# Four modulation vectors moved from the tensor engine to the vector engine, with the first LayerNorm and the first loads reordered

## The chip, the cores and the metric

The kernel runs on one core of one Trainium2 chip. The metric is the device time of one execution in microseconds (us). Times are medians, with the range in brackets. The profile and the trace are those of one execution of each kernel, so a number read from them can differ from the median of the runs by a few tenths of a per cent.

Engines: PE is the tensor engine, ACT the scalar engine, DVE the vector engine, POOL is GpSimd, SP is the engine that only issues transfers. ACT can issue transfers too. In these traces an issue that takes long holds up what stands behind it on the same engine (9.59 us on ACT's queue, below). The granted clock is the share of PE's full clock that the profile records as allowed; at half clock it is 0.5 (so from 15 to 28 us in the kernel before).

## The reference, cut to what matters

```python
mod = (silu(c) @ w_mod).reshape(1, 6, 1, 640)      # c: 1x640, w_mod: 640x3840
sa, ca, ga, sb, cb, gb = mod[:, 0], ..., mod[:, 5]
h = layernorm(x) * (1 + ca) + sa                   # x: 2048x640
x = x + ga * attention(h, k_cache, v_cache, wq, wo)   # 32 heads of 128, 2048 keys
h = layernorm(x) * (1 + cb) + sb
x = x + gb * block_B(h)                            # a small gated MLP block
```

Attention is nearly all of the work: 32 heads times 4 chunks of 512 queries, 128 steps, each with 8 softmax exponentials of 128x1024. The vectors `sa` and `ca` are needed at once. The vectors `ga`, `sb`, `cb` and `gb` are needed only after most of the attention is done.

## The kernel before

The kernel does not write its instructions in program order. It records operations with an estimated duration and a priority, and a small planner at the top of the file simulates the five engines and decides the order in which each engine gets its instructions. Two of its lines are part of the change:

```python
            t_eng[e] = s + o.dur                      # when the engine is free again
            ...
            for u in o.succ:                          # when a successor may start
                u.ready = max(u.ready, (o.end if o in u.deps else o.start) + u.slack + (...))
```

The four late vectors are computed on PE: `silu(c)` is broadcast to 128 columns (`s_bc`), and each vector is ten matmuls, whose result stands on all 128 partitions at once. The vector `ga` is made in the first 30 us, the other three inside steps 17 to 22.

```python
    def modulation(p, hf, w_ap, w_t, pool, key, prio):
        ...
        for k in range(KT):
            P.op("PE", lambda e, k=k: e.matmul(m[:, 0:HD], s_bc[:, k, :], w_ap[:, k, sl], ...), ...)
        P.op("DVE", lambda e: e.tensor_scalar_add(out=mod[p][hf].ap, in0=m[:, 0:HD], ...), ...)
    ...
    dma("ACT", lambda e: e.dma_start(pre_ap, mod_src(2)), 800, ...)        # weights of ga, 800 KB
    ...
    load_v(0, -296.5, "ACT", after=(ln0[1],))                              # V of head 0, on ACT's queue
    ...  # for head 1:
            load_v(h, (-293, -290, -289.5)[h - 1], "ACT" if h == 1 else "SP", ...)
```

ACT's queue also issues the load of the second chunk of x (in `ln1`, called "the x load" below) and the rest of the first `wq`. On the same engine, behind these issues, stand two of the five copies that turn the first normalised chunk into `hT`, the input of the first query projection.

At the far end of the attention, DVE and POOL share the residual work. For chunks 2 and 3 the sum `x1 = tmp + xb` is on DVE, while POOL multiplies and adds other tiles in chains. Both inputs of these operations are in SBUF. The result `x1` is stored in the space of `hT`, so the profile shows the sum as `f_hT<-f_tmp,f_y`.

```python
                if hf:
                    tt("DVE" if ch > 1 else "POOL", x1[t].ap, w.ap, xb[t].ap, ALU.add, ...)
```

Of the kernel before, what the change touches and what calls it, by code (L numbers as in the profile page):

```python
# [40 lines left out]
class Plan:  # L41
# [3 lines left out]
    ENG = ("PE", "ACT", "DVE", "POOL", "SP")  # L45
    FIRST = {"PE": 100000, "ACT": 100000, "DVE": -6, "POOL": 100000, "SP": -5}
# [43 lines left out]
    def schedule(self):  # L90
# [20 lines left out]
        while len(self.all) < len(self.ops):  # L111
            best = None
            for e in self.ENG:
                st = []
                for o in avail[e]:
                    if e == "PE" and o is not pe[pe_i]:
                        continue
                    r = o.ready
                    if not all(free[t.pool] for t in o.newps):
                        continue  # L120
                    r = max([r] + [min(free[t.pool])[0] for t in o.newps])
                    st.append((max(r, t_eng[e]), o.prio, o.seq, o))
                if not st:
                    continue
                lim = min(st)[0] + 30.0
                c = min((x for x in st if x[0] <= lim), key=lambda x: x[1:3])
                if best is None or c[0] < best[0]:
                    best = c
            assert best is not None, ("stuck", pe[pe_i].prio, [d.eng for d in pe[pe_i].deps if not hasattr(d, "end")])
            s, o = best[0], best[3]  # L130
            e = o.eng
            avail[e].remove(o)
            if e == "PE":
                pe_i += 1
            for t in o.newps:
                b = min(free[t.pool])
                free[t.pool].remove(b)
                t.bank, t.ap = b[1], self.pools[t.pool][b[1]]
                for d in b[2]:
                    o.deps.setdefault(d, False)  # L140
            o.start = s
            t_eng[e] = s + o.dur
            self.busy[e] += o.dur
            if o.dma:
                t = max(dma_t[e], s + o.dur)
                both = min(max(0.0, max(dma_t[x] for x in self.ENG if x != e) - t), o.kb * 1024 / 190.0)
                dma_t[e] = t + both + (o.kb * 1024 - 190.0 * both) / 380.0
                o.end = dma_t[e] + 2000.0
            else:
                o.end = s + o.dur + o.lat  # L150
            o.idx = len(self.seq[e])
            self.seq[e].append(o)
            self.all.append(o)
            for pool, bank in o.gives:
                free[pool].append((o.end, bank, (o,)))
            for u in o.succ:
                u.ndep -= 1
                u.ready = max(u.ready, (o.end if o in u.deps else o.start) + u.slack + (1500.0 if o.dma and u.eng in ("DVE", "ACT") and not u.dma else 0.0))
                if u.ndep == 0:
                    avail[u.eng].append(u)  # L160
            for t in o.ptiles:
                left[t] -= 1
                if left[t] == 0:
                    last = {}
                    for r in t.refs:
                        if r.eng not in last or r.idx > last[r.eng].idx:
                            last[r.eng] = r
                    free[t.pool].append((max(r.end for r in t.refs), t.bank, tuple(last.values())))
# [104 lines left out]
def fast_path(nc, es, flag, A_x, A_k_cache, A_v_cache, A_wq, A_wo, B_w1, B_w2, B_w3, B_w4, c, w_mod, out):  # L273
# [8 lines left out]
    G4 = D // 4  # L282
# [119 lines left out]
    for i in range(NKV - 1):  # L402
        v_ones(i)
# [47 lines left out]
    P.op("POOL", lambda e: e.tensor_copy(s_bc.ap, c_f.ap.unsqueeze(2).to_broadcast([128, KT, 128])), 1000, (c_f,), (s_bc,), -290, lat=300)  # L451
    spin(50, -298)
    for k in range(KT):
        def mcol(e, k=k):
            for j in range(2 * KT):
                ins = e.matmul(mc[:, j:j + 1], wm_ap[:, k, j * 128:(j + 1) * 128], s_bf[:, k:k + 1],
                               start=(k == 0 and j == 0), stop=(k == KT - 1), skip_group_check=True)
                if k < KT - 1:
                    dummy(e, 1)
            return ins  # L460
        P.op("PE", mcol, 2 * KT * (85 if k < KT - 1 else 62), (wm[k], s_bf, ones), (mc,) + ((warm,) if k < KT - 1 else ()), -290 + k, accum=True)
# [23 lines left out]
    def ln_stats(src, src_t, g, i, prio, slack=0.0):  # L485
        s = st[n_st[0] % NST]
        n_st[0] += 1
        for hf in range(2):
            P.op("DVE", lambda e, hf=hf: e.bn_stats(s[:, hf * 6:hf * 6 + 6], src[:, hf * HD:(hf + 1) * HD]), 485, src_t, (s,), prio, slack=slack)  # L489
        P.op("DVE", lambda e: e.bn_aggr(mv_ap[g][:, i, :], s.ap), 200, (s,), (mvs[g][i],), prio)  # L490
# [29 lines left out]
    def normed(dst, dst_t, src, src_t, g, i, fp, prio):  # L520
        P.op("DVE", lambda e: e.tensor_scalar(out=dst, in0=src, scalar1=mv_ap[g][:, i, 0:1], scalar2=rs_ap[g][:, i:i + 1],
                                              op0=ALU.subtract, op1=ALU.mult),
             445, src_t + (mvs[g][i], rs[g]), (dst_t,), prio)
# [23 lines left out]
    def ln1(ch, prio):  # L547
        g = ln_slot()
        if ch == 1:
# [3 lines left out]
                640, (), xs + held, -296.7, after=(wm_load[3], ln0[1]))  # L553
# [3 lines left out]
        for a, z in ((0, 2), (2, 4)) if ch < 2 else ((0, 4),):  # L557
            for i in range(a, z):
                ln_stats(xs[i].ap, (xs[i],) + held, g, i, prio, 0.0 if ch == 0 else 2000.0)
            if ch == 0:  # L560
                ln0.append(rstd_act(g, a, z, prio - 100))
            else:
                rstd_dve(g, a, z, prio - 1)
            for i in range(a, z):
                normed(xn[i].ap, xn[i], xs[i].ap, (xs[i],) + held, g, i, False, prio - 1)
        raw = [T() for _ in range(4)]
        if ch == 0:
# [5 lines left out]
            for i in range(4):  # L573
                def tr(e, i=i):
                    for k in range(KT):
                        ins = e.transpose(hslice(k, i, i + 1), xn[i][:, k * 128:(k + 1) * 128], ident_t[:])
                    return ins
                P.op("PE", tr, 330, (xn[i], ident), (hp[0], hp[1], hq, hp[4]), (-286.6 if i < 2 else -280) + 0.1 * i, accum=True)
# [44 lines left out]
    def modulation(p, hf, w_ap, w_t, pool, key, prio):  # L623
        m = Tile(pool=pool)
        sl = slice(hf * HD, (hf + 1) * HD)
        for k in range(KT):
            P.op("PE", lambda e, k=k: e.matmul(m[:, 0:HD], s_bc[:, k, :], w_ap[:, k, sl], start=(k == 0), stop=(k == KT - 1)),  # L627
                 MM(HD), (s_bc,) + w_t, (m,), key(k), accum=True)
        P.op("DVE", lambda e: e.tensor_scalar_add(out=mod[p][hf].ap, in0=m[:, 0:HD], scalar1=1.0 if p == 4 else 0.0),
             490, (m,), (mod[p][hf],), prio)  # L630

    mod_src = lambda p: w_mod[:, p * D:(p + 1) * D].rearrange("(k p) n -> p k n", p=128)
    pre_ap = KV_t[:, (NKV - 1) * KVW:(NKV - 1) * KVW + KT * D].rearrange("p (k n) -> p k n", k=KT)
    pre_t = tuple(K[NKV - 1]) + (V[NKV - 1],)
    dma("ACT", lambda e: e.dma_start(pre_ap, mod_src(2)), 800, (wm[3],), pre_t, -297, after=(ln0[0],))
    for hf in range(2):
        modulation(2, hf, pre_ap, pre_t, "O%d" % hf, lambda k, hf=hf: 0.5 + hf + 0.01 * k, -50)
    v_ones(NKV - 1)
    load_v(0, -296.5, "ACT", after=(ln0[1],))

    def load_head(h):
# [3 lines left out]
        if h in (1, 2, 3):  # L645
            load_k(h, (-294, -291, -289)[h - 1], (wm[2],), () if h < 3 else from_slot(12))
            load_v(h, (-293, -290, -289.5)[h - 1], "ACT" if h == 1 else "SP", () if h == 1 else (wm[2],), after=(ln0[1],) if h == 1 else ())
# [15 lines left out]
    MS = 17  # L663
    for n, p in enumerate((4, 3, 5)):
        dma("SP", lambda e, n=n, p=p: e.dma_start(w_half[n % 2], mod_src(p)), 800, (), (W12[n % 2],) + (w2b if n == 1 else ()) + tuple(wm),
            MS * NP - 30 + n, from_slot((MS + 2 * n) * NP - 20))
        for hf in range(2):
            modulation(p, hf, w_half[n % 2], (W12[n % 2],) + (w2b if n == 1 else ()), "M",
                       lambda k, i=2 * n + hf: NP * (MS + i) + 4.65 + k, NP * MS - 60)

# [10 lines left out]

    def q_proj(s, keys):
        g, ch, hh = of_step(s)
        q = QT[s % 3]
        m = Tile(pool="M")
        for i, kk in enumerate((0, 2, 1, 4, 3)):
            P.op("PE", lambda e, i=i, kk=kk: e.matmul(m.ap, wq_t[g % 2][:, kk, hh * 128:(hh + 1) * 128], hT_t[ch][:, kk, :],  # L687
                                                      start=(i == 0), stop=(i == KT - 1)),
                 MM(QC), (wq[g % 2][hh], hT[ch][kk]), (m,), keys[i], accum=True)
        P.op("DVE", lambda e: e.tensor_copy(q.ap, m.ap), 690, (m,), (q,), s * NP - 90)  # L690
# [45 lines left out]
    def step(s):  # L736
# [11 lines left out]
        for j in range(NP):  # L748
# [4 lines left out]
            for r in range(2):  # L753
                kt = 2 * j + r
                P.op("PE", lambda e, sp=sp, r=r, kt=kt: e.matmul(sp[:, r * QC:(r + 1) * QC], K_ap[b][:, kt * 128:(kt + 1) * 128], q.ap, start=True, stop=True),  # L755
                     MM(QC), (K[b][kt // 4], q), (sp,), n + (0.307 if 9 <= s < 112 else 0.01) * r, accum=True)
# [96 lines left out]
    dma("SP", lambda e: e.dma_start(w_half[0], B_w1.rearrange("(k p) n -> p k n", p=128)), 800, (), (W12[0],), E)  # L853
    w2_rows = B_w2.rearrange("(g r) n -> r g n", g=4)
    dma("SP", lambda e: e.dma_start(w_half[1][:, 0:4, :], w2_rows[0:128]), 640, (), (W12[1],), E)
    for g in range(4):
        dma("SP", lambda e, g=g: e.dma_start(w_half[1][g * 32:(g + 1) * 32, 4, :], w2_rows[128:G4, g, :]), 40, (), (w2b[g],), E)
# [885 lines left out]
```

## Time and profile before

| what | value | where |
|---|---|---|
| time | 1386.88 us (1386.02 to 1386.93), 3 runs | times |
| span of the profiled run | 1386.3 us | page, head |
| PE busy | 1371.0 us, 99% | page, part 1 |
| longest PE wait | 6.6 us, for ACT's copies | waits |
| granted clock, 14 to 30 us | 0.57 | windows |

PE is the engine to watch. From the page of the kernel before, part 1 (busy us of each engine, share of the span, number of instructions) and part 4 (the chain that ended last, by engine):

```profile
PE 1371.0 (99%) x13128; PEld 944.9 (68%) x13128; DVE 540.3 (39%) x1402; ACT 1101.7 (79%) x1143; POOL 101.9 (7%) x89
...
PE 97%; DVE 2%; ACTq 1%; ACT 0%; issue 0%; POOL 0%; POOLq 0%
```

From the stretches view (window, its length, then for each engine the busy time and the number of instructions in the order PE, PEld, DVE, ACT, POOL, then the granted clock, the DMA share and GB/s):

```profile
14.00:30.00 16.00, 8.56 (x31) 3.57 (x32) 2.95 (x6) 4.54 (x6) 0.13 (x1) 0.57 1.33 212
...
160.00:235.00 75.00, 75.00 (x744) 52.49 (x742) 24.42 (x61) 63.16 (x62) 0.00 (x0) 1.00 0.39 89
...
1150.00:1215.00 65.00, 63.27 (x636) 43.68 (x635) 45.85 (x122) 55.30 (x75) 38.36 (x33) 1.00 0.31 69
```

PE is full from 30 us on. It is badly used only from 14 to 30 us, where it was busy for 8.56 of 16 us and at little more than half the clock. The reason is in the timeline of ACT (start, duration, line and operation; ACTq marks an issue):

```profile
7.90 0.39 ACTq L635 DMA_DIRECT2D f_KV<-in_w_mod_dram  x1
...
10.15 0.38 ACTq L552 DMA_DIRECT2D f_y<-in_A_x_dram  x1
10.57 9.59 ACTq L605 DMA_DIRECT2D f_KV<-in_A_v_cache_dram  x2
20.20 0.78 ACT L581 ACTIVATE f_hT<-f_O,f_small 128x512 bf16<-128x512 bf16 x1 [9.85 <-issue]
```

The other issues in this stretch took 0.38 to 0.54 us. The two V loads took 9.59 us together, of which the second took 8.99 (11.17 to 20.16), and the first `hT` copy of ACT began only when they were done. PE waited for it; the waits view of PE from 10 to 30 us says:

```profile
PE f_M L687 <- ACT f_hT L581: 6.6, 1, 6.6
```

(The numbers are the total, the count and the longest wait, in us.) The line view of the modulation's matmuls (count, then the shortest, median and longest duration in ns, first and last start) shows what the four vectors cost PE:

```profile
L627 PE MATMUL f_M<-f_W,f_sbc x30: 299/299/300, 183.6 to 238.2; 128*128 128x320 bf16 x30
...
L627 PE MATMUL f_O<-f_KV,f_sbc x10: 474/474/475, 24.1 to 27.4; 128*128 128x320 bf16 x10
```

The ten of `ga` fell in the half-clock stretch, the other thirty at full clock into steps 17 to 22.

Last, the tail, which matters later: the timelines of DVE and of POOL of the kernel before near 1187 us.

```profile
1184.69 4.54 POOL L528 TENSOR_TENSOR f_y<-f_y,f_mod 128x640 f32<-128x640 f32 x3
1189.34 2.18 POOL L536 TENSOR_SCALAR f_xn<-f_y,f_small 128x640 bf16<-128x640 f32 x2
1191.49 2.11 POOL L528 TENSOR_TENSOR f_y<-f_y,f_mod 128x640 f32<-128x640 f32 x1
...
1187.05 0.69 DVE L690 CAST f_PQ<-f_M 128x512 bf16<-128x512 f32 x1
...
1188.05 1.86 DVE L528 TENSOR_TENSOR f_hT<-f_tmp,f_y 128x640 bf16<-128x640 f32 x1
...
1190.87 1.32 DVE L528 TENSOR_TENSOR f_hT<-f_tmp,f_y 128x640 bf16<-128x640 f32 x1
```

DVE casts the next query tile (`f_PQ<-f_M`) first and does the sum of tile 8 after it. The sum took 1.86 us, although the same sum takes 0.82 us when POOL is idle. Nobody waits for the sum here, so it costs nothing. The next sum, at 1190.87, shows that the waiting goes both ways: it took 1.32 us, and POOL's operation beside it (1191.49) took 2.11 us where 1.54 is usual.

### The profile page before, as it was taken

What the parts mean: (1) busy time and instruction counts of PE and PEld (TensorE: products, weight loads), DVE (VectorE), ACT (ScalarE), POOL (GpSimd) and SP (SyncE); (2) the same over time, 40 slices, a digit from 0 to 9 for tenths busy, and PEclk for the clock granted to TensorE, in tenths of its full rate; (3) what the DMA queues carried; (4) which work ended last, traced back from release to release, by engine and by line L of the source; (5) the groups of instructions that cost most, each with busy time, mean ns of one, the idle gap of its engine ahead of it and who ended that gap; (6) DMA issues with size and microseconds to landing.
All of it is one profiled execution on the core that took longest, in us unless ns stands there. A gap on an engine that the chain in (4) does not pass through costs nothing.

```text
span 1386.3 us, 29857 instructions
## 1 busy us (share of the span) xinstructions
PE 1371.0 (99%) x13128; PEld 944.9 (68%) x13128; DVE 540.3 (39%) x1402; ACT 1101.7 (79%) x1143; POOL 101.9 (7%) x89
## 2 busy tenths in 40 slices
PE   7999999999999999999999999999999999999999
PEld 5667776777677777777777677777676766655665
DVE  4553323223322332333233323332333245897663
ACT  3988888888898889888988888888888888833322
POOL 0000000000000000000000000000333236500000
PEclk8999999999999999999999999999999999999999
DMA  9460624242223412051125122432226101331220
GB/s 233 98 124 24 122 79 94 35 88 54 47 35 56 86 32 50 19 97 32 43 36 107 35 47 36 73 69 47 55 51 134 38 17 24 105 83 20 57 49 31
DMA packets 259164, 88.91 MB, mean 64 GB/s; under 512 B 236689, under 2 KB 257746, under 8 KB 259026
## 3 DMA queue, kind: packets, MB, share of 16 engines
q1 hardware_dynamic: 252498, 82.92, 30.4%
q10 hardware_dynamic: 6528, 4.00, 1.3%
q8 instruction: 105, 1.72, 0.5%
q14 instruction: 33, 0.27, 0.1%
HBM read 43.48 MB, written 2.62 MB: 33 GB/s over the span
## 4 chain that ended last, share of the span: by engine, by line
PE 97%; DVE 2%; ACTq 1%; ACT 0%; issue 0%; POOL 0%; POOLq 0%
PE f_O L774 33%; PE f_S L755 32%; PE f_M L687 10%; PE f_M L712 10%; PE f_S L951 2%; PE f_M L951 2%; PE f_S L938 2%; PE f_O L938 2%; PE f_S L889 1%; PE f_S L912 1%; PE f_M L912 1%; ACTq L605 1%; PE f_O L889 1%; DVE f_small L489 0%; PE f_M L627 0%; PE f_S L431 0%
## 5 line engine op out<-in xcount | busy, mean ns | idle before, releaser
L757 ACT ACTIVATE f_PQ<-f_S 128x1024 bf16<-128x1024 f32 x1024 | 1041.3, 1024 | 147.5 <-PE f_S L755 134.6
L774 PEld LDWEIGHTS f_O<-f_KV,f_PQ 128*128 128x128 bf16 x8192 | 589.6, 98 | 231.6 <-DVE f_OO L783 2.1
L755 PE MATMUL f_S<-f_PQ,f_KV 128*128 128x512 bf16 x2048 | 727.8, 380 | 1.0 <-DVE f_PQ L690 0.8
L774 PE MATMUL f_O<-f_KV,f_PQ 128*128 128x129 bf16 x8192 | 712.9, 220 | 1.3 <-DVE f_OO L783 1.3
L720 DVE TENSOR_TENSOR f_y<-f_M,f_y 128x320 f32<-128x320 f32 x192 | 94.3, 491 | 536.4 <-PE f_M L712 536.4
L712 PE MATMUL f_M<-f_wo,f_OO 128*128 128x320 bf16 x992 | 272.8, 299 | 0.0
L755 PEld LDWEIGHTS f_S<-f_PQ,f_KV 128*128 128x128 bf16 x2048 | 197.0, 98 | 31.8 <-DVE f_PQ L690 1.5
L687 PE MATMUL f_M<-f_hT,f_wq 128*128 128x512 bf16 x640 | 176.8, 380 | 7.5 <-ACT f_hT L581 6.6
L712 PEld LDWEIGHTS f_M<-f_wo,f_OO 128*128 128x128 bf16 x992 | 96.1, 98 | 28.5
L690 DVE CAST f_PQ<-f_M 128x512 bf16<-128x512 f32 x128 | 88.4, 691 | 63.2 <-PE f_M L687 63.1
L783 DVE TENSOR_TENSOR f_OO<-f_O,f_rl 128x256 bf16<-128x256 f32 x256 | 108.4, 423 | 8.2
L687 PEld LDWEIGHTS f_M<-f_hT,f_wq 128*128 128x128 bf16 x640 | 62.3, 98 | 72.0 <-ACT f_hT L581 7.4
L528 POOL TENSOR_TENSOR f_y<-f_y,f_mod 128x640 f32<-128x640 f32 x32 | 49.6, 1559 | 820.0 <-DVE f_y L720 819.9
L781 DVE RECIPROCAL f_rl<-f_O 128x2 f32<-128x2 f32 x256 | 43.3, 169 | 36.6 <-PE f_O L774 32.5
L718 DVE COPY f_y<-f_M 128x320 f32<-128x320 f32 x32 | 15.7, 490 | 64.2 <-PE f_M L712 64.2
L941 ACT ACTIVATE f_OO<-f_O 128x512 bf16<-128x512 f32 x28 | 16.7, 596 | 26.9 <-PE f_O L938 26.8
L941 ACT ACTIVATE f_OO<-f_S 128x512 bf16<-128x512 f32 x28 | 16.7, 596 | 24.9 <-PE f_S L938 24.9
L489 DVE BATCH_NORM_STATS2 f_small<-f_y 128x6 f32<-128x320 f32 (+1 forms) x72 | 33.0, 480 | 2.0 <-POOL f_y L528 2.0
L534 ACT ACTIVATE f_xn<-f_y,f_small 128x640 bf16<-128x640 f32 x10 | 9.0, 914 | 30.5 <-DVE f_small L513 30.5
L951 PE MATMUL f_M<-f_KV,f_OO 128*128 128x320 bf16 x224 | 31.7, 299 | 0.0
L951 PE MATMUL f_S<-f_KV,f_OO 128*128 128x320 bf16 x224 | 31.7, 299 | 0.0
L951 PEld LDWEIGHTS f_M<-f_KV,f_OO 128*128 128x128 bf16 x224 | 21.9, 98 | 8.9
(137 smaller groups left out, 507.8 us busy)
## 6 DMA issues: line engine op xcount, KB each, us to landing
f_KV<-in_A_v_cache_dram SPq DMA_DIRECT2D x30, 512.0 KB, 4.8
f_wo<-in_A_wo_dram SPq DMA_DIRECT2D x8, 640.0 KB, 4.2
f_wq<-in_A_wq_dram SPq DMA_DIRECT2D x7, 640.0 KB, 5.7
f_xin<-in_A_x_dram SPq DMA_DIRECT2D x13, 320.0 KB, 3.7
f_W<-in_w_mod_dram SPq DMA_DIRECT2D x3, 800.0 KB, 4.8
out_dram<-f_xin SPq DMA_DIRECT2D x15, 160.0 KB, 1.8
f_KV<-in_B_w_dram SPq DMA_DIRECT2D x5, 432.0 KB, 3.3
f_KV<-in_A_k_cache_dram SPq DMA_TRANSPOSE x128, 2.7
```

The costliest lines, as they stand in the source:

```text
L528: P.op(eng, lambda e: e.tensor_tensor(out=out, in0=a, in1=b, op=op), COST[eng][0], rd, wr, prio, lat=300 if eng == "POOL" else None)
L687: P.op("PE", lambda e, i=i, kk=kk: e.matmul(m.ap, wq_t[g % 2][:, kk, hh * 128:(hh + 1) * 128], hT_t[ch][:, kk, :], start=(i == 0), stop=(i ...
L690: P.op("DVE", lambda e: e.tensor_copy(q.ap, m.ap), 690, (m,), (q,), s * NP - 90)
L712: P.op("PE", lambda e, m=m, qt=qt, hf=hf, hh=hh: e.matmul(m[:, 0:HD], OT_ap[gs][:, qt, hh, :], wo_t[g % 2][:, hh, hf * HD:(hf + 1) * HD], ...
L720: P.op("DVE", lambda e, m=m, yt=yt: e.tensor_tensor(out=yt.ap, in0=m[:, 0:HD], in1=yt.ap, op=ALU.add), 490, (m, yt), (yt,), s * NP - 60)
L755: P.op("PE", lambda e, sp=sp, r=r, kt=kt: e.matmul(sp[:, r * QC:(r + 1) * QC], K_ap[b][:, kt * 128:(kt + 1) * 128], q.ap, start=True, stop ...
L757: x = P.op("ACT", lambda e, sp=sp, pt=pt: e.activation(pt.ap.rearrange("p k q -> p (k q)"), sp.ap, ACT.Exp, scale=SCALE), 1021, (sp,), (pt ...
L774: ins = e.matmul(o[bk][:, w * 129:w * 129 + 129], pt[:, r, qt * 128:(qt + 1) * 128], V_ap[b][:, u, 0:129], start=(u == 0 and w == 0), stop ...
L781: P.op("DVE", lambda e, ov=ov, i0=i0: e.reciprocal(rl_t[:, i0:i0 + 2].unsqueeze(2), ov[:, 0:258].rearrange("p (u d) -> p u d", u=2)[:, :, ...
L783: evac.append(P.op("DVE", lambda e, ov=ov, i0=i0, bk=bk: e.tensor_tensor(out=On_ap[gs][:, 2 * bk:2 * bk + 2, hh, :], in0=ov[:, 0:258].rear ...
L938: P.op("PE", lambda e, m=m, f=f, kk=kk: e.matmul(m.ap, w3_ap[:, kk, f * 128:(f + 1) * 128], nT_ap[ch][:, kk, :], start=(kk == 0), stop=(kk ...
L951: P.op("PE", lambda e, f=f, hf=hf: e.matmul(m[:, hf * 512:hf * 512 + HD], gT_ap[:, f, i * 128:(i + 1) * 128], w4_ap[f][:, hf * HD:(hf + 1) ...
```

## The change

The intent is to take the late vectors off PE, where each matmul is on the critical path, and give them to DVE, which is idle more than half of the time. `w_mod` is loaded transposed by the DMA, so that a vector is a row-wise product with `silu(c)` and a sum over the row, and its 640 results stand one per partition, in five columns. They go to DRAM and come back broadcast to all partitions. This also frees the 800 KB load from the start. Besides, V of head 1 goes to SP, the LayerNorm of the first chunk takes all four statistics before its normalisations, the transposes of the first chunk are recorded one by one, the first query projection is split into halves that ACT and DVE cast in parallel, and 20 of the 40 dummy matmuls set between those of the first modulation vectors are left out (80 others stay). Two lines of the planner get a new model of how instructions on DVE and ACT overlap.

```diff
+    LAP = {"DVE": 80.0, "ACT": 100.0}
...
-            t_eng[e] = s + o.dur
+            t_eng[e] = s + (o.dur if o.dma else max(o.dur - self.LAP.get(e, 0.0), 60.0))
...
-                u.ready = max(u.ready, (o.end if o in u.deps else o.start) + u.slack + (...))
+                u.ready = max(u.ready, (o.start if o not in u.deps else t_eng[e] + 45.0 if e == u.eng and e != "PE" and not o.dma and not u.deps[o] else o.end) + u.slack - (45.0 if e == u.eng and e in self.LAP and not o.dma else 0.0) + (...))
...
             dma("ACT", lambda e: e.dma_start(y_t[:, 4:8, :]..., x2d[512:1024, :]...),
-                640, (), xs + held, -296.7, after=(wm_load[3], ln0[1]))
+                640, (), xs + held, -294, after=(wm_load[3], ln0[1]))
...
-    def modulation(p, hf, w_ap, w_t, pool, key, prio):
-        ... # ten matmuls and two copies per vector
-    dma("ACT", lambda e: e.dma_start(pre_ap, mod_src(2)), 800, (wm[3],), pre_t, -297, after=(ln0[0],))
+    def modulation(n, p, slot):
+        for j in range(KT):
+            dmaT(... e.dma_start_transpose(w_half[i][:, j, :].unsqueeze(1), w_mod[:, p * D + j * 128:p * D + (j + 1) * 128]) ...)
+            P.op("DVE", ... e.tensor_tensor(out=tmp[j % 2].ap, in0=w_half[i][:, j, :], in1=s_row.ap, op=ALU.mult), 825, ...)
+            P.op("DVE", ... e.tensor_reduce(out=col[:, j:j + 1], in_=tmp[j % 2].ap, op=ALU.add, ...), 825, ...)
+        dma("SP", lambda e: e.dma_start(m_scr.ap()[n].rearrange("(j q) -> q j", q=128), col.ap, allow_slow_non_contiguous=True), ...)
+        dma("SP", lambda e: e.dma_start(mod_t[p][:], m_scr.ap()[n:n + 1, :].to_broadcast([128, D])), ...)
...
-            load_v(h, (-293, -290, -289.5)[h - 1], "ACT" if h == 1 else "SP", ...)
+            load_v(h, (-292, -290, -289.5)[h - 1], gate=(wm[2],))
...
+        halves = ((m, 0, QC),) if s else ((m, 0, QC // 2), (Tile(pool="S1"), QC // 2, QC))   # first query projection
```

The priority of the x load goes from -296.7 to -294, and V of head 0 keeps -296.5 (the lower number stands ahead in ACT's queue); the two `hT` copies stand behind both.

## The prediction

> **What bounds the kernel now.** The page gives PE 1371.0 of 1386.3 us busy; the chain that ended last is 97% PE. By stretches PE is 100% busy from 30 to 1000 us, with ScalarE (ACT) near 88% and VectorE (DVE) at 31 to 43%. Beyond the first 30 us PE idles about 5 us in all. So only PE work taken out and the start can move the time.
>
> **The start before.** In the timeline the last first-LayerNorm transposes end at 12.9 us and three of five hT copies (DVE) by 14.4, but the two on ACT begin only at 20.20: ACT's queue spent 11.17 to 20.16 (8.99 us) issuing the second V load behind 800 KB of modulation weights, wq, x and V of head 0. PE waits 6.6 us for them (waits view). The granted clock is 0.50 from 14.4 to 28.0, so the q projection, the first scores (23.29) and two modulation groups (5 matmuls, 1.33 us each) run at half speed. The second q projection starts at 28.43.
>
> **Removed.** (a) The 8.99 us issue wait: V of head 1 goes to SP, the 800 KB load goes. (b) Tiles 2 and 3 of xn could be normalised at 10.35 but stood on DVE behind the copies of sa and ca until 11.64; now all statistics come first, then four normalisations. (c) Two modulation groups at half clock, 2.66 us. (d) Six at full clock in steps 17 to 22: the period there is 9.93 us, without them about 9.26; 4.0 us in all, where PE has no idle.
>
> **Added.** 20 multiplies and 20 reductions of 128x640 on DVE; estimates from the trace: 0.82 us and 0.81 (a 512-wide reduce took 0.68): 33 us, one pair per step, in a DVE gap of 4.6 us (203.7 to 208.75), so none should reach PE. 20 weight transposes at 1.27 us of SP issue and small DMAs, at 27 to 47% DMA share: hidden.
>
> **New start, estimated from those durations.** Statistics done 9.0, normalisation 10.6, transposes 11.1, hT 12.6, half casts and first scores 13.5 instead of 23.3. V of head 0 lands near 16, about when needed. The second q projection starts near 15.7 instead of 28.4: 12.7 us.
>
> **Sum.** 12.7 + 4.0 = 16.7 us; I give back 0.2 net for a half-clock window that may still fall in 11 to 18 us[...] or a short wait for V. Prediction 1370.4 us, 1.2% faster; 8 in 10 between 1366.5 and 1375.5. Faster by over 2%: 0.02; within 2%: 0.97; slower by over 2%: 0.01.
>
> **What would show it.** ACT's hT copies begin near 11 us; first scores 13 to 14.5; second q projection 15 to 18; PE at 100% in 160 to 260 us without waits on DVE; PE busy down some 7 us; a period of 9.26 us in steps 17 to 22; no half-clock stretch over 4 us.
>
> **What would make it wrong.** ACT's queue still stalling before the hT copies; K tiles or V of heads 0 and 1 landing late, so PE gives back 2 to 6 us in steps 0 and 1; the clock staying at half after 14 us; a DVE multiply stuck on a late weight transpose, holding up the O copies and PE.
>
> [...]

The forecast's sum is 12.7 + 4.0 less 0.2, or 16.5 us, which takes 1386.9 to 1370.4 us. The cuts marked in it are words on why the clock falls, which no trace of this case shows; no term of the sum is cut. Some supposed causes that were not shown are cut from the expectations below in the same way; their times stand as they were recorded.

## The result, and the profile after

| | before | after |
|---|---|---|
| time | 1386.91 us (1386.02 to 1387.01), 4 runs | 1380.16 us (1378.93 to 1380.4), 4 runs |
| span of the profiled run | 1386.3 us | 1378.8 us |
| ratio after / before | | 0.9951, 95% interval 0.9934 to 0.9968 |

A ratio is the mean time of one kernel's fast runs over the mean of the other's of the same rounds, so it is not quite the ratio of the medians. All outputs are right. The change gains 0.5%. The predicted 1370.4 us and its range (1366.5 to 1375.5) were missed by 10 and by 5 us; the class, within 2%, was right.

To see where the time went, take the start of the first exponential of each of the 128 steps in both traces and subtract. The difference is the lead of the kernel after (steps are counted from 0, so 126 is the last but one):

| at step | lead, us | what happened since the line above |
|---|---|---|
| 1 | 8.03 | the start; predicted was 12.7 |
| 17 | 8.03 | nothing lost, although DVE makes the first vector in this time |
| 24 | 12.10 | steps 17 to 23 gained 4.07; predicted was 4.0 |
| 119 | 12.10 | nothing lost, although DVE makes the other three |
| 125 | 12.58 | small shifts |
| 126 | 5.29 | 7.29 lost within one step |
| end of the run | 7.5 | span 1386.3 less 1378.8; some 2 us come back after step 127 |

So the middle went exactly as predicted, and there are two faults: the start gained 4.7 us too little, and one step near the end lost 7.3 us that the prediction does not mention.

**The middle.** From the groups by form, 100 to 300 us, of the kernel after (busy us, mean ns of one, idle time before):

```profile
L639 DVE TENSOR_TENSOR f_tmp<-f_W,f_nTx 128x640 f32<-128x640 bf16 x19 | 15.7, 826 | 3.8 <-ACT f_PQ L772 3.8
L641 DVE TENSOR_REDUCE f_small<-f_tmp 128x1 f32<-128x640 f32 x19 | 15.6, 820 | 28.7 <-ACT f_PQ L772 28.7
```

The durations are those that the prediction estimated (0.82 and 0.81 us), and from 170 to 320 us the waits view has no wait of PE at all. The page's first part is now:

```profile
PE 1354.2 (98%) x12839; PEld 941.6 (68%) x13073; DVE 573.6 (42%) x1435; ACT 1101.5 (80%) x1144; POOL 100.2 (7%) x88
```

DVE has 33 us more, as predicted. That PE has 16.8 us less proves nothing: weight loads fell by 55 and matmul records by 289, although each matmul has a weight load, so some 230 matmul records are missing from this trace. The lead per step does not have this fault.

**The start.** The timeline of ACT in the kernel after:

```profile
8.91 0.39 ACTq L605 DMA_DIRECT2D f_KV<-in_A_v_cache_dram  x1
9.33 3.84 ACTq L553 DMA_DIRECT2D f_y<-in_A_x_dram  x1
13.29 0.78 ACT L581 ACTIVATE f_hT<-f_O,f_small 128x512 bf16<-128x512 bf16 x1 [4.17 <-DVE f_hT L585]
```

The long issue has not gone. It moved from the V load to the x load, and shrank from 8.99 to 3.84 us. The `hT` copies of ACT start at 13.29 and not near 11. PE's waits from 10 to 30 us, and the stretch from 14 to 30 us:

```profile
PE f_M L697 <- ACT f_hT L581: 1.8, 1, 1.8
```

```profile
14.00:30.00 16.00, 14.63 (x104) 8.04 (x107) 7.24 (x30) 11.73 (x14) 0.00 (x0) 0.79 1.21 186
...
1150.00:1215.00 65.00, 59.40 (x538) 40.13 (x546) 50.65 (x130) 46.83 (x63) 27.79 (x25) 0.95 0.32 74
```

The clock still fell to half, from 14.99 to 21.81 us, and the second query projection ran in it: 18.90 to 21.04 (critical view), where the prediction had it near 15.7.

**The late step.** The last line above already shows that from 1150 to 1215 us PE is busy 3.9 us less than before and the mean clock is 0.95. The waits view of PE from 1160 to 1200 us, then the timelines of POOL and DVE, and the chain of waits of the kernel after:

```profile
PE f_M L727 <- DVE f_PQ L701: 4.4, 1, 4.4
```

```profile
1172.77 6.02 POOL L529 TENSOR_TENSOR f_y<-f_y,f_mod 128x640 f32<-128x640 f32 x4
...
1173.86 5.62 DVE L529 TENSOR_TENSOR f_hT<-f_tmp,f_y 128x640 bf16<-128x640 f32 x1
1179.40 0.68 DVE L701 CAST f_PQ<-f_M 128x512 bf16<-128x512 f32 x1
```

```profile
1173.94 5.53 DVE f_hT L529
1179.47 0.61 DVE f_PQ L701
...
1180.13 0.98 PE f_M L727 x3
```

The sum of tile 8 took 5.62 us. Beside it POOL ran four operations back to back, unslowed (6.02 us for four is 1.5 each, as in the kernel before). The query cast now stands behind the sum on DVE, and PE waited for it. The clock was at half from 1178.93 for 6.83 us. PE stood still until 1180.13, so 5.6 us of work fell into that stretch. A pair of score matmuls took 0.85 us in it and 0.43 us after it, so the stretch cost 2.8 us; with the wait of 4.4 us that is 7.2 of the 7.3 us. Some of it comes back: from the start of step 127 to the end the kernel after takes 180.65 us and the kernel before 182.60.

### The profile page after: what moved, and what is told of

Same layout as the page of the kernel before. It is cut to its first block, busy times and chain, and to the rows that moved or that the text cites. A ratio compares the mean times of both kernels' runs of the same rounds, so it can differ in the third digit from the quotient of the medians.

```text
span 1378.8 us, 29615 instructions
## 1 busy us (share of the span) xinstructions
PE 1354.2 (98%) x12839; PEld 941.6 (68%) x13073; DVE 573.6 (42%) x1435; ACT 1101.5 (80%) x1144; POOL 100.2 (7%) x88
## 3 DMA queue, kind: packets, MB, share of 16 engines
HBM read 41.68 MB, written 2.63 MB: 32 GB/s over the span
## 4 chain that ended last, share of the span: by engine, by line
PE 97%; issue 1%; DVE 1%; ACT 0%; ACTq 0%; POOL 0%; POOLq 0%
PE f_O L789 35%; PE f_S L770 30%; PE f_M L697 10%; PE f_M L727 10%; PE f_S L966 2%; PE f_M L966 2%; PE f_O L953 2%; PE f_S L953 2%; PE f_S L904 1%; PE f_S L927 1%; PE f_M L927 1%; PE f_O L904 1%; DVE f_hT L529 0%; ACTq L553 0%; DVE f_small L490 0%
## 5 line engine op out<-in xcount | busy, mean ns | idle before, releaser
L770 PE MATMUL f_S<-f_PQ,f_KV 128*128 128x512 bf16 x1856 | 666.5, 380 | 4.7 <-ACT f_PQ L705 0.9
L697 PE MATMUL f_M<-f_hT,f_wq 128*128 128x512 bf16 (+1 forms) x610 | 171.2, 380 | 4.0 <-ACT f_hT L581 1.8
L733 DVE COPY f_y<-f_M 128x320 f32<-128x320 f32 x32 | 15.7, 492 | 50.8 <-PE f_M L727 50.8
L641 DVE TENSOR_REDUCE f_small<-f_tmp 128x1 f32<-128x640 f32 x20 | 16.4, 820 | 30.3 <-ACT f_PQ L772 30.3
```

The costliest lines, as they stand in the source:

```text
L697: P.op("PE", lambda e, i=i, kk=kk, mm=mm, a=a, z=z: e.matmul(mm[:, 0:z - a], wq_t[g % 2][:, kk, hh * 128:(hh + 1) * 128], hT_t[ch][:, kk, ...
L770: P.op("PE", lambda e, sp=sp, r=r, kt=kt: e.matmul(sp[:, r * QC:(r + 1) * QC], K_ap[b][:, kt * 128:(kt + 1) * 128], q.ap, start=True, stop ...
```

## The experiments

Two questions were tested. For the start: is the loss due to the issue that holds ACT's queue behind a V load, or to the bytes that are in flight at that time, whoever issues them? For the late step: is it due to the planner's new lines, which changed the order on DVE, or to the modulation work on DVE? A third came up on the way: what the round trip through DRAM costs. Each run has 4 fast runs in 3 rounds (the last has 6 in 5), with runs of the kernel before on the same chip.

| run | time, us | ratio to before | 95% interval |
|---|---|---|---|
| lap_on_before2 | 1391.19 | 1.0028 | 1.0011 to 1.0045 |
| lap_off2 | 1375.5 | 0.9917 | 0.99 to 0.9933 |
| x_late2 | 1376.7 | 0.9926 | 0.9909 to 0.9942 |
| x_first2 | 1379.63 | 0.9948 | 0.9932 to 0.9965 |
| mod_only | 1379.69 | 0.9945 | 0.9929 to 0.9962 |
| pool_break | 1374.82 | 0.9908 | 0.9892 to 0.9925 |
| add_behind | 1373.35 | 0.9897 | 0.9881 to 0.9914 |
| best1 | 1377.32 | 0.9931 | 0.9915 to 0.9948 |
| both | 1373.1 | 0.9893 | 0.9877 to 0.991 |
| both_sp | 1376.03 | 0.9924 | 0.9908 to 0.9941 |
| both_v3 | 1371.98 | 0.9891 | 0.9874 to 0.9907 |
| both_shift | 1379.94 | 0.995 | 0.9937 to 0.9963 |

The change itself is 0.9951.

### lap_on_before2: the planner's lines alone, in the kernel before

```diff
+    LAP = {"DVE": 80.0, "ACT": 100.0}
-            t_eng[e] = s + o.dur
+            t_eng[e] = s + (o.dur if o.dma else max(o.dur - self.LAP.get(e, 0.0), 60.0))
...   # and the line of u.ready, as in the change; nothing else
```

> The kernel before with only the planner's new cost model (the two LAP lines), nothing else of the change. Its DVE order around the first x1 add of chunk 2 becomes the order of the changed kernel: the add stands ahead of the q cast. Theory P (the add[...] is locked out by a chain of four POOL operations, and the planner's order puts it there): one DVE add of about 5.6 us near 1180 us, one PE wait of 4 to 4.5 us behind it, a half clock stretch of 6.8 us, and 1390 to 1393 us, slower than before by 4 to 6 us. Rival R (the late loss comes from the modulation or from the earlier start, not from the planner): no such wait, 1386 to 1388 us.

The kernel became slower: 1391.19 us against 1387.09 of the kernel before in the same rounds. The timelines of POOL and DVE in this run:

```profile
1184.75 6.04 POOL L529 TENSOR_TENSOR f_y<-f_y,f_mod 128x640 f32<-128x640 f32 x4
...
1185.86 5.61 DVE L529 TENSOR_TENSOR f_hT<-f_tmp,f_y 128x640 bf16<-128x640 f32 x1
1191.39 0.68 DVE L691 CAST f_PQ<-f_M 128x512 bf16<-128x512 f32 x1
```

It is the picture of the kernel after, to 0.02 us, without any modulation on DVE. PE waits 4.4 us for the cast here too, and the lead over the kernel before stays within 0.7 us until step 125. The half-clock stretch there was 3.41 us and not 6.8, and 5.96 us were lost in step 126; from step 127 on the run takes 180.66 us, as the kernel after does, so 1.9 us come back; in all the span grew by 3.3 us in the profiles and the median by 4.1. So the planner's lines alone make the late loss, and the DVE work of the modulation is not needed for it.

### lap_off2: the kernel after with the planner's old lines

```diff
-            t_eng[e] = s + (o.dur if o.dma else max(o.dur - self.LAP.get(e, 0.0), 60.0))
+            t_eng[e] = s + o.dur
...   # and the old line of u.ready
```

> The changed kernel with the planner's old cost model, all else kept. The DVE order there has the q cast ahead of the add. Theory P: the PE wait of 4.4 us near 1175 us is gone, the clock stays at 1.0 there, and the time is 1374 to 1376.5 us (12.1 us of gain at step 125 kept but for what the kernel before also lost in the tail). Rival R: the wait stays and the time is 1379 to 1381.

1375.5 us (1374.07 to 1375.62), and the lead of 13.06 us at step 25 is held. From the timelines of POOL and DVE:

```profile
1171.63 4.54 POOL L529 TENSOR_TENSOR f_y<-f_y,f_mod 128x640 f32<-128x640 f32 x3
...
1173.98 0.69 DVE L701 CAST f_PQ<-f_M 128x512 bf16<-128x512 f32 x1
...
1174.99 1.87 DVE L529 TENSOR_TENSOR f_hT<-f_tmp,f_y 128x640 bf16<-128x640 f32 x1
```

The order is again cast first, sum after, and POOL has three operations in the chain and not four. PE does not wait. By the ratios (0.9951 less 0.9917) the two planner lines cost about 4.7 us of 1387, by the run before (0.0028) about 3.9. The prediction has no term for them.

One more thing can be read from these timelines. The sum ends 0.68 us after POOL's chain does: here the chain ends at 1171.63 + 4.54 = 1176.17 and the sum at 1176.86; in the run before 1190.79 and 1191.47; in the kernel after 1178.79 and 1179.48; in the kernel before 1189.23 and 1189.91. The sum takes 0.82 us undisturbed. In all four it did nearly all of its work only after POOL had paused. POOL was not slowed in that time (6.02 us for four operations in the kernel after), and DVE's other work beside it kept its duration: in `lap_off2` the statistics took 0.48 us at 1172.88 and the product `f_tmp<-f_M,f_mod` 0.48 us at 1174.59, both inside the chain, and 0.48 and 0.49 us at 1180.64 and 1182.61, when POOL had stopped. Here and in the kernel before, the sum began within POOL's last operation of the chain and waited for the rest of that one, 1.18 us. In the run before and in the kernel after it began within the first of four and waited through the other three as well, 4.93 us.

### pool_break and add_behind: is it the back-to-back chain?

`pool_break` changes no order on any engine. It only makes POOL's third operation of the chain wait until DVE's sum is done, so that POOL has nothing ready after its second.

```diff
-                    tt("POOL", b.ap, b.ap, mod_t[3][:], ALU.add, (b,) + tuple(mod[3]), (b,), prio)
+                    tt("POOL", b.ap, b.ap, mod_t[3][:], ALU.add, (b,) + tuple(mod[3]), (b,), prio, need=(lambda: x1_add[8],) if t == 6 else ())
```

> The changed kernel with one wait more and every engine's order kept: the third of the four chained POOL operations (the add of tile 6) waits for DVE's x1 add of tile 8. Theory P [...]: the DVE add is let in after the second POOL operation and takes 2.4 to 2.9 us instead of 5.62; the PE wait falls from 4.4 to some 1.2 to 1.7 us; 1375.5 to 1378.5 us. Rival (the add is slow by itself or by something else, and POOL's work beside it is a coincidence): still about 5.6 us, POOL now stands still for it, 1379.5 us or more.

```profile
1175.49 3.04 POOL L531 TENSOR_TENSOR f_y<-f_y,f_mod 128x640 f32<-128x640 f32 x2
1179.36 3.04 POOL L531 TENSOR_TENSOR f_y<-f_y,f_mod 128x640 f32<-128x640 f32 x2 [0.82 <-DVE f_hT L531]
...
1176.59 2.63 DVE L531 TENSOR_TENSOR f_hT<-f_tmp,f_y 128x640 bf16<-128x640 f32 x1
```

The sum took 2.63 us and ended 0.69 us after POOL's second operation, although POOL's first ended within its wait as well. So the sum did not get in at the seam of these two POOL operations (where one ends and the next begins), and it did get in as soon as POOL had nothing to run. This is not so at every seam: in the kernel before, the sum at 1190.87 got in between POOL's scaling (TENSOR_SCALAR, one tile as input, ended 1191.52) and the TENSOR_TENSOR recorded right behind it, and ended 0.67 us after the first, while the second took 2.11 us; in `lap_off2` the sum at 1177.81 took 1.32 us and POOL's TENSOR_TENSOR beside it 2.11 us too. The 7 seams at which the timelines above show a sum passed over (three in the kernel after, three in `lap_on_before2`, one in `pool_break`) all lie between two TENSOR_TENSOR. Why the two kinds differ no run shows.

PE's wait for the cast fell from 4.4 to 1.4 us. Time 1374.82 us (1373.6 to 1377.21), a little better than expected. The profiled run is the slowest of the four: PE stood still for 2.16 us until 186.7, with no releaser but "issue", a half-clock stretch of 3.41 us followed, and some 4 us of lead were lost there. The two fastest runs have a mean granted clock of 1.000, so nothing of the kind.

`add_behind` does the opposite: it keeps POOL's chain and lets DVE's sum wait for its end, so that the planner puts the cast first.

```diff
+                    tt(..., need=(lambda: pool_end[7],) if t == 8 else ())     # the sum of tile 8
...
+                    pool_end[t] = tt("POOL", b.ap, b.ap, mod_t[3][:], ALU.add, ...)
```

> The changed kernel, planner's new cost model kept, in which DVE's x1 add of tile 8 depends on the last of the four chained POOL operations, so that the planner puts the q cast and the modulation multiply ahead of it on DVE. Theory P: no DVE add over about 2.5 us, no PE wait over 1 us at 1170 to 1190 us, no half clock there; 1373.5 to 1376.5 us. Rival: PE would have waited there for something else (the O copies, the banks of the output projection): 1378 us or more.

1373.35 us (1371.9 to 1375.67). The two sums in the timeline, at 1180.27 and 1182.56, take 0.82 and 0.81 us, PE does not wait for the cast, and nothing is lost at step 126. With the planner's new lines still in, one dependence takes the late loss away.

### x_late2 and x_first2: the issue behind the V load

`x_late2` makes the x load follow the two `hT` copies on ACT; `x_first2` puts it ahead of V of head 0.

```diff
# x_late2
-                640, (), xs + held, -294, after=(wm_load[3], ln0[1]))
+                640, (), xs + held, -294, after=(wm_load[3], ln0[1], hT_act[-1]))
# x_first2
-                640, (), xs + held, -294, after=(wm_load[3], ln0[1]))
+                640, (), xs + held, -297.5, after=(wm_load[3], ln0[1]))
```

> The changed kernel with the load of x chunk 1 issued on ACT's queue after the two hT copies, not between V of head 0 and them; nothing else. Theory Q (ACT's queue stands still for 3.84 us on the issue behind the 2048-row V load, which delays hT[...]): hT copies on ACT start at 10.9 to 11.3 us instead of 13.29, first scores 13.2 to 14 instead of 16.12, second q projection 15.5 to 17.5 instead of 18.9; 1376 to 1378.5 us, the late wait unchanged. Rival S (the start is bound by what the DMAs bring, K tiles and V of head 0 at 17.8): hT early, but the first output matmuls no earlier than before, time 1379.5 to 1381.

> The changed kernel with x chunk 1 issued on ACT's queue ahead of V of head 0: the same loads, bytes and queue, only these two swapped, so no issue follows the V load before the hT copies. Theory Q: no issue over 0.6 us before the hT copies, which start at 10.9 to 11.3; V of head 0 lands later, near 20 to 21 us instead of 17.8, and PE then waits for it, so most of the gain goes: 1378.5 to 1381 us. Rival (the queue stalls by the bytes outstanding on it, whatever the order): the V issue itself takes some 3 to 4 us and the hT copies start at 13 again.

The timeline of ACT in `x_late2`, then in `x_first2`, and the longest wait of PE in `x_first2` from 10 to 60 us:

```profile
11.67 0.78 ACT L582 ACTIVATE f_hT<-f_O,f_small 128x512 bf16<-128x512 bf16 x1 [2.56 <-PE f_O L578]
11.79 1.30 ACTq L554 DMA_DIRECT2D f_y<-in_A_x_dram  x1
```

```profile
8.91 0.39 ACTq L553 DMA_DIRECT2D f_y<-in_A_x_dram  x1
9.34 0.52 ACTq L605 DMA_DIRECT2D f_KV<-in_A_v_cache_dram  x1
```

```profile
PE f_O L789 <- DMA f_KV<-in_A_v_cache_dram: 2.5, 1, 2.5
```

In `x_late2` the copies start at 11.67, the first scores come at 14.21 (16.12 in the kernel after), there is no half-clock stretch at the start, and the lead after step 1 is 11.90 us against 8.03. That is the predicted start to within 0.8 us, with copies and scores a little later than expected for this run. The time is 1376.7 us (1375.66 to 1377.43); the late wait of 4.4 us is still there, and 1.05 us are lost in steps 3 to 5, with waits of 0.3 us for a K tile at 40.9 and of 0.4 us for DVE's O copies at 51.7. The x load itself landed no later (19.84 us, 20.80 in the kernel after), but the planner had also reordered SP's queue and DVE in places.

In `x_first2` both issues are short, since nothing stands behind the V load, and the copies start as early. But now V of head 0 lands at 20.55 and not at 17.8 us, and PE waits 2.5 us for it and 1.7 us more at 54. So both answers hold: the issue behind the V load holds the queue (3.84 us in the kernel after), and moving the 640 KB ahead of V is paid for in bytes. The free place is behind the copies.

The trace gives a regularity for the length of the hold. The issue that follows a V load ended within 1 us of the landing of the transfer that stood ahead of the V load on the same queue: 20.16 and 20.35 us in the kernel before, 13.18 and 13.02 in the kernel after, 13.09 and 12.93 in `x_late2`; the widest is 13.40 and 12.41 in `lap_off2`. A V load is 2048 rows of 256 bytes. What the issue waits for no run shows.

### mod_only: the modulation alone, in the kernel before

```diff
   # the new s_rows and modulation, with their calls, in place of the old ones; V of head 1 stays on ACT's queue,
   # LayerNorm, first projection and planner as in the kernel before
```

> The kernel before with the modulation part of the change alone: four vectors on VectorE from transposed weights, old planner, old LayerNorm order, V of head 1 still on ACT's queue. Theory: 4.0 to 4.1 us gained in steps 17 to 23 as in the changed kernel; at the start the issue of V of head 1 now ends when x chunk 1 lands, near 15.5 to 16.5 us instead of 20.16, and two modulation groups are gone: second q projection at 22 to 24.5 us instead of 28.4; no late wait, as the old planner is kept; 1376.5 to 1379 us. Rival (the added DVE work or the transposes stall PE somewhere and give some of it back): PE waits on DVE in steps 12 to 30 and over 1380 us.

1379.69 us (1379.19 to 1380.61), just above what was expected. The lead is 5.33 us after the start, as the 800 KB load is gone; steps 17 to 23 bring 4.08 us; there is no late wait. About 2 us are lost in steps 6 to 11, where PE waits once for ACT (1.4 us at 115.5) while `silu(c)` makes its way through DRAM (98.4 to 119.8 us). This hinted at a cost of the round trip, but the kernel after makes the same two transfers (95.4 to 113.0 us) and loses nothing there; it was not taken further in this run.

The modulation alone is thus as fast as the whole change (0.9945 and 0.9951, with overlapping intervals): what the other parts add at the start (8.03 us of lead against 5.33), the planner's lines lose again near the end. No run takes the LayerNorm order or the split projection alone.

### best1: old planner lines and a later x load

```diff
   # planner's lines as before the change, and
-                640, (), xs + held, -294, after=(wm_load[3], ln0[1]))
+                640, (), xs + held, -294, after=(wm_load[3], ln0[1], half[0]))     # half[0]: ACT's cast of the first half query
```

> The changed kernel with both causes taken away: the planner's old cost model, and x chunk 1 issued on ACT's queue after the hT copies and the half cast of q. If theories P and Q are the whole of the loss and add: 1371 to 1373.5 us, hT copies on ACT near 11.2 to 11.8 us, first scores near 13.7 to 14.2, no PE wait over 1.2 us after 20 us, i.e. 1.0 to 1.15% faster than before. If they overlap (a third wait, such as the transposes of hT chunk 1, takes their place): 1374 to 1375.5.

A miss: 1377.32 us (1377.02 to 1378.77). The start leads by 11.86 us and nothing is lost late. But the planner put K tiles of head 3 ahead of the transposes of the second chunk on SP's queue, PE waited 2.3 us for that chunk until 43.4, the clock fell to half for 3.4 us, and 4.79 us were lost in step 4. A repair of one queue had moved the wait to another.

### both, both_sp and both_v3: the two repairs together

`both` is `x_late2` and `add_behind` in one. `both_sp` issues the x load on SP behind the K tiles of head 0. `both_v3` is `both` with the V load of head 3 held until step 1, so that the transposes of the second chunk are not behind it:

```diff
# both_v3 against both
-            load_v(h, (-292, -290, -289.5)[h - 1], gate=(wm[2],))
+            load_v(h, (-292, -290, -289.5)[h - 1], gate=(wm[2],), need=() if h < 3 else from_slot(16))
# both_sp against add_behind
-            dma("ACT", lambda e: e.dma_start(y_t[:, 4:8, :]..., x2d[512:1024, :]...), 640, (), xs + held, -294, after=(wm_load[3], ln0[1]))
+            dma("SP", lambda e: e.dma_start(y_t[:, 4:8, :]..., x2d[512:1024, :]...), 640, (), xs + held, -294.1, after=(ln0[1],))
```

> Both repairs in one kernel: the x load issued on ACT's queue behind the two hT copies, and the DVE add of tile 8 made dependent on the last addition of the GpSimd chain. If the two losses are separate, they add: head gain about 11.9 us less the 1.05 that the late x load cost in steps 3 to 5, plus 4.1 in steps 17 to 23, no late loss: 1370.5 to 1373.5 us, ratio near 0.989. If the half-clock stretch of the head and the late add share a cause, or the slack found in one is eaten by the other, the time stays near add_behind's or x_late2's, 1373 to 1377.

> As the run before it, but the x load is issued by SyncE behind the four K tiles of head 0, so that it is at its old place in time (near 12 us) and never on ACT's queue, and the transposes of chunk 1 keep their place on SyncE's queue. ACT's hT copies should start near 11.7, first scores near 14.3, no loss in steps 3 to 5 (these cost 1.05 us in x_late2): 1369.5 to 1372.5 us. If what counts is the bytes ahead of V of head 0 and not the queue that issues them, V lands late as in x_first2 and PE waits up to 2.5 us at 20.6: 1372 to 1375.

> As the first run of this call, with one difference: the V load of head 3 is held until step 1, so that it goes behind the four transposes of chunk 1 on SyncE's queue (2048 rows, the issue behind it took 3.2 to 4.1 us). Those transposes are then done some 3 to 4 us sooner than in x_late2 (39.6), the waits at 40.9 and 51.7 go, and the 1.05 us lost in steps 3 to 5 come back: 1369.5 to 1372.5 us. If the loss had another cause, it is as the first run within 0.5 us, or V of head 3 is late and PE waits near 50 us.

`both_v3` has the lowest median, 1371.98 us (1371.32 to 1373.31), 1.1% under the kernel before, and its ratio interval lies clear of that of the change. `both` has 1373.1 (1370.96 to 1373.77). The intervals of these two and of `add_behind` overlap, so the runs do not prove that the repair of the start adds anything on top of the late one. Single profiles point to it: the lead at step 6 is 10.10 us in `both`, 10.85 in `x_late2` and 11.21 in `both_v3`, and 8.03 to 9.46 in four with the start of the change (the kernel after, `add_behind`, `pool_break`, `lap_off2`). `both_sp` was a miss at 1376.03 us (1374.6 to 1377.97): PE waits 2.9 us for K tiles and 2.0 us for DVE's O copies in the first 60 us, and the lead is down to 7.65 us by step 6.

With ACT's queue free, the second K tile of head 0 becomes the next thing to arrive late, and its landing varies between runs: 13.58 us in the profile of `both`, 15.65 in `both_v3`, 15.85 in `both_sp`, 17.34 in the run that follows, with PE gaps of 0, 0.8, 1.3 and 2.1 us for it. That variation was not studied further.

### both_shift: the round trip through DRAM one to two steps later

In the profile of `both_v3` PE stands still for 1.33 us until 183.98, with no releaser but "issue", and four other profiles with the new modulation (`both`, `best1`, `pool_break`, `add_behind`) have the like; of these, two do not have the repaired start, so the count in the expectation below is not exact. The vector's write to DRAM and its broadcast are close by. This run moves only those two transfers, on SP's queue; the orders on PE, ACT and DVE are the same.

```diff
-        dma("SP", ... m_scr.ap()[n].rearrange("(j q) -> q j", q=128), col.ap ..., slot + 24.0)
+        dma("SP", ... m_scr.ap()[n].rearrange("(j q) -> q j", q=128), col.ap ..., slot + 72.0, from_slot(slot + 72))
-        dma("SP", ... mod_t[p][:], m_scr.ap()[n:n + 1, :].to_broadcast([128, D]) ..., slot + 24.0)
+        dma("SP", ... mod_t[p][:], m_scr.ap()[n:n + 1, :].to_broadcast([128, D]) ..., slot + 72.0)
```

> As both_v3, with one difference: the write of each finished modulation vector to DRAM and its broadcast back go out one to two steps later on SyncE's queue; the orders on the tensor, vector and scalar engines are the same. In both_v3 the profile has the PE stall 1.33 us at 183.98, put down to 'issue', 4.0 us after the first broadcast was issued (179.99); five of eight profiles with the new modulation and a repaired head have such a stall of 1.1 to 2.2 us, 3.5 to 5.1 us after that issue. If the scattered write and its broadcast cause it, there is no stall at that place and, if there is one, it follows the moved broadcast: median within 1 us of both_v3's, 1370 to 1372.5. If the cause lies in the program's place there[...], the stall stays at the same matmul near 184 us. If no stall is seen anywhere this one profile leaves it open, and the five rounds only say whether the time falls by the 1.3 us.

The median was a miss, 1379.94 us (1376.75 to 1383.42), and the profile tells why. The stall at 184 us is gone. In its place PE waits at 247 and 251 us, 4.6 us of lead are lost in steps 24 to 27, and another 1.4 by step 42; some 3 us more than in `both_v3` were lost at the start, to the late K tile and 3.4 us at half clock. The second vector's write now stands directly ahead of the next `wq` load and of the transposes of O. The timeline of SP and PE's waits from 244 to 256 us:

```profile
235.92 0.36 SPq L648 DMA_DIRECT2D m_scratch<-f_small  x1
236.33 0.53 SPq L611 DMA_DIRECT2D f_wq<-in_A_wq_dram  x1
236.90 13.86 SPq L715 DMA_TRANSPOSE f_OO<-f_OO  x4
```

```profile
PE f_M L730 <- DMA f_OO<-f_OO: 2.3, 1, 2.3
PE f_S L774 <- ACT f_PQ L776: 1.9, 1, 1.9
```

Four such transposes took 5.21 us to issue at 53.41 us in the kernel after; here they took 13.86. The DMA view of this run in three windows that follow each other, 235 to 237.5, 237.5 to 248 and 248 to 250.5 us, gives the packets:

```profile
DMA packets 656, 0.00 MB, mean 1 GB/s; under 512 B 656, under 2 KB 656, under 8 KB 656
```

```profile
DMA packets 185, 0.19 MB, mean 18 GB/s; under 512 B 0, under 2 KB 185, under 8 KB 185
```

```profile
DMA packets 1012, 0.60 MB, mean 239 GB/s; under 512 B 557, under 2 KB 1012, under 8 KB 1012
```

The write's 640 elements go out in these 656 packets, all under 512 bytes and 0.00 MB together, in under a microsecond. Then, for 10.5 us, all that follows crawls at 18 GB/s, and after that it runs at 239. The same pair shows at the first vector: the issues part of the DMA view (size, median us to landing) from 160 to 200 us has the `wo` load 1 us behind the write in `both_v3`, and with the write moved away in `both_shift`:

```profile
f_wo<-in_A_wo_dram SPq DMA_DIRECT2D x1, 640.0 KB, 14.5
...
m_scratch<-f_small SPq DMA_DIRECT2D x1, 2.5 KB, 12.8
```

```profile
f_wo<-in_A_wo_dram SPq DMA_DIRECT2D x1, 640.0 KB, 4.3
```

So the write cost the load issued behind it about 10 us (14.5 us to landing against 4.3), and in the second case the transposes 8.7 us of issue (13.86 against 5.21). The write itself, of 2.5 KB, landed 12.8 us after its issue in `both_v3`, 9.2 in `both_shift`, and 11.2 and 8.7 in the kernel after. In the kernel after, where PE has no wait from 170 to 320 us, it is free: its `wo` load takes 13.3 us there and is not waited for. Whether the stall of 1.3 us at 184 us belongs to the same cause is not shown. It went when the transfers moved, but that is one profile, six of the eleven others with the new modulation have no such stall either, and what PE lacked there the trace does not show. That part stays open.

## Why the prediction was wrong

**What bounds the kernel.** "So only PE work taken out and the start can move the time." This step failed. PE is full because its feeders are on time, and an order change on one feeder moved the time by 7.3 us in one step at 1174 us. The prediction went through the named parts of the change and did not cost the two planner lines. They are in the diff, and the order of DVE's instructions near the end (the sum of tile 8 ahead of the query cast) could have been read without a run. `lap_on_before2` and `lap_off2` show that these lines alone make the late wait, at 3.9 to 4.7 us of the median; `pool_break` and `add_behind` show that the sum was held as long as POOL had the next TENSOR_TENSOR of its chain ready (5.62 us beside four of them, 2.63 us when the chain was cut after two, 0.82 us behind it).

**The start.** "(a) The 8.99 us issue wait: V of head 1 goes to SP, the 800 KB load goes." The mechanism was named rightly, and it was listed among what would make the prediction wrong, but the size was off: the wait shrank to 3.84 us and did not go, since the x load took the place behind a V load. The term of 12.7 us measured 9.53 at its own mark, the second query projection (28.43 to 18.90), and 8.03 once the half-clock stretch was over. `x_late2`, with that one issue moved, measured 11.90. Not all of the difference is the hold itself: in `pool_break` ACT's copies are as late (13.36 us), but its clock did not fall at the start, and it led by 10.38 us at step 1. By these single profiles some 1.5 us are the hold and some 2.4 us the half clock that came with it. The prediction asked which loads leave the queue; the question was what stands behind the V load that stays.

**The half clock.** "I give back 0.2 net for a half-clock window that may still fall in 11 to 18 us" did not cover it. In the kernel after the clock fell to 0.50 at 14.99, and again at 1178.93, near the end of the late wait, each time for 6.83 us. What makes it fall the traces do not show. The half-clock stretches lasted 13.65 us in the kernel before, 6.83 us twice in the kernel after, and 10.24 and 3.41 us in `lap_on_before2`; these are one, two, three and four times 3.41 us to within 0.01; why, no run shows. The order of the instructions does not settle it: the kernel after, `add_behind` and `pool_break` have the same order on every engine until the last steps, and their mean clock from 14 to 30 us was 0.79, 0.79 and 1.00. Nor did PE stand idle before the falls at the start: in the 3.41 us before them (as long as the shortest stretch) it was busy for 2.02 us, or 59%, in the kernel before and for 1.50 us, or 44%, in the kernel after, and in the kernel before the clock fell at 14.39, when the wait of 6.6 us was about to begin (14.43). No threshold comes out of these traces: in `x_first2` PE waited 2.5 us at one stretch for V of head 0, and the mean clock from 14 to 30 us was 1.00.

The fall at the start went with late copies, though not always. With ACT's `hT` copies at 13.29 us or later it came in six of seven profiles (mean clock from 14 to 30 us 0.57 in the kernel before, 0.79 in the kernel after, `add_behind` and `mod_only`, 0.68 in `lap_on_before2`, 0.89 in `lap_off2`; 1.00 in `pool_break`), with copies before 12 us in one of seven (0.89 in `both_shift`; 1.00 in `x_late2`, `x_first2` and `best1`, and 1.0 over the whole run in `both`, `both_sp` and `both_v3`). The dummy matmuls that the change leaves out do not decide it: seven profiles without them have no fall at the start, and `mod_only`, which keeps them, has one of 6.83 us. This luck is part of the spread between the runs of one kernel: the two fastest of `add_behind` (1371.9 and 1372.19 us) have a mean granted clock of 1.000, the two others (1374.51 and 1375.67) of 0.997 and 0.998.

**Right.** The LayerNorm: statistics were done at 8.6 us (9.0 predicted), transposes at 10.9 (11.1). The middle: 4.07 us against 4.0, the period of steps 18 to 22 is 9.25 us against 9.26, the products and sums took 0.826 and 0.820 us, and PE did not wait on DVE. The DMA side was called "hidden"; in the kernel after it is, but `both_shift` shows that this depends on the place, not on the DMA share that the prediction argued from.

With both faults repaired, `both_v3` runs in 1371.98 us, inside the range that was predicted for the change. It is another kernel, so this does not make the prediction right.

## What to carry to other kernels

Cost every line of a diff, also those that only steer the order of instructions, and compare the order on each engine before predicting. When a long issue sits on a compute engine's queue, ask which transfer it stands behind (here a V load: 3.84 and 8.99 us), and put the copies that PE waits for ahead of it. Where PE waits behind a DVE sum of two SBUF tiles, keep that sum away from back-to-back TENSOR_TENSOR chains on POOL (0.82 us became 5.62 here), and keep scattered writes to DRAM away from any load that is wanted within 10 us (18 GB/s for 10.5 us here).
